# Contractions over 448 rows in chunks of 128, 128, 128 and 64 instead of four of 112, in a fused attention and spatial-gating block

## The chip, the cores and the metric

The kernel runs on one core of a Trainium2 chip. The metric is the device time of one execution in microseconds (us). A run also reports the mean clock that TensorE was granted, as a share of full speed, and a state: slow when it lies over 1.5% above the fastest run of the same kernel, else fast. Comparisons use fast runs; a quoted median is of all runs, and where slow ones are among them the text says so. Where a ratio is quoted, it is the mean time of one kernel's fast runs over that of the other's fast runs of the same rounds, so it isn't quite the ratio of the medians quoted beside it. Engines are called as in the profile: PE (TensorE matmuls), PEld (its weight loads), DVE (VectorE), ACT (ScalarE), POOL (GpSimd), SP (SyncE, which issues all transfers but that of the vector `c`).

## The reference, cut to what matters

```python
# x: 1 x 2048 x 448;  D = 448, 16 heads of 28, a causal window of 256
mod = (silu(c) @ w_mod).reshape(1, 6, 1, 448)        # sa, ca, ga, sb, cb, gb
h = layernorm(x) * (1 + ca) + sa
x = x + ga * A(h)       # qkv = h @ wqkv; masked softmax(q k^T / sqrt(28)) v; @ wo
h = layernorm(x) * (1 + cb) + sb
x = x + gb * B(h)       # z = gelu(h @ w_in); g = w_sp @ layernorm(z2) + b_sp; (z1 * g) @ w_out
```

Every product with `w_mod`, `wqkv` and `wo` contracts over D = 448 rows. Each is done as four matmuls that accumulate into one result. How 448 is split over the four is what the change alters. In the second half (`B`) the split over 448 was 128, 128, 128, 64 already, and there the left-over 64-row matmuls are few.

## The kernel before

A planner lays out all operations per engine from a list of priorities, and emits each engine's program with semaphores. The parts that matter, with cuts marked:

```python
KP = 112; KC = 4                              # 448 = 4 x 112
WARM = (15, 5)                                # warm-up matmuls: at the start, behind the modulation
# ...
def wload(name, prio, dst, w, a, b, o=None, ks=(0, KC), eng="sp"):
    src = w[ks[0] * KP:ks[1] * KP, a:b].rearrange("(c p) n -> p c n", p=KP)
    return load(name, prio, lambda e: e.dma_start(dst[0:KP, ks[0]:ks[1], o:o + b - a], src), ...)
# ...  modulation columns: 448 x 1 results, in groups of four one-column matmuls
for kc in range(KC):
    last = mm(e, ps[0:w, b, 4 * i + mc:4 * i + mc + 1],
              wmod_sb[0:KP, kc, v * D + mc * KP:v * D + mc * KP + w],
              sc_sb[0:KP, kc:kc + 1], kc == 0, kc == KC - 1)
# ...  queries and keys: 48 groups of four
return mm(e, ps[:, ten.slot, 0:n], WQK[0:KP, kc, 4 * g:4 * g + 4, :].rearrange("p a b -> p (a b)"),
          hT[0:KP, kc, t0 * 128:t1 * 128], kc == 0, kc == KC - 1)
# ...  values: 16 groups
return mm(e, ps[:, ten.slot, 0:D], hT[0:KP, kc, t * 128:(t + 1) * 128], wv_sb[0:KP, kc, :], kc == 0, kc == KC - 1)
# ...  attention output: 16 groups
return mm(e, ps[:, wt.slot, 0:D], oT[0:KP, oTt.slot, kc, :], wo_sb[0:KP, kc, :], kc == 0, kc == KC - 1)
```

The softmax here doesn't subtract the row's maximum and nothing guards it: scores larger than these inputs give would overflow.

## Time and profile before

| | before |
|---|---|
| time, median (range), in the runs of the comparison | 283.23 us (282.51 to 283.36) |
| span of the profiled run, granted clock | 280.8 us, 0.999 |
| PE busy | 268.1 us |
| first / last exponential starts | 16.02 / 112.84 us |
| changes of TensorE's tile shape, in program order | 123 |

How to read it: three stretches follow each other. Up to 16 us the inputs land, the modulation is computed and the first queries and keys are projected. From there to the last exponential (90 of them on ACT) is the attention. The rest is the second half, almost pure TensorE. The profile's lines stand in the prediction. The row that is last counts how often the next matmul uses a tile of another shape than the one before (128, 64 or 32 rows; in 3 of the 123 cases only the columns differ). The text calls this a mode change; by the records of this run, one between row counts adds 91 to 96 ns (medians) to the spacing of two starts. Scores run on 32 rows (the heads are padded to 32), nearly everything else on 112 or 128, which count as one shape: a matmul of 128 rows starts as soon behind one of 112 as behind another of 128 (at 448 columns 189 ns in both cases).

### The profile page before, as it was taken

The numbers are of one execution on the slowest core, as the hardware profiler recorded it, in microseconds if no ns is written. First come the engines' busy times: TensorE is split into PE (matmuls) and PEld (weight loads), VectorE is DVE, ScalarE is ACT, GpSimd is POOL, SyncE is SP. The second block draws the span as 40 slices with busy tenths as digits, with TensorE's granted clock in tenths as the row PEclk, the third lists the DMA queues.
The fourth block names the chain that finished last, engine by engine and source line by source line (L and its number), as shares of the span: only waits on it lengthen the run. The fifth ranks groups of instructions, "written<-read, shape, count | busy, mean of one in ns | idle before, by whom it ended". The sixth has DMA issues, their size and how long they took to land.

```text
span 280.8 us, 6444 instructions
## 1 busy us (share of the span) xinstructions
PE 268.1 (95%) x2669; PEld 136.8 (49%) x2684; DVE 173.1 (62%) x439; ACT 128.1 (46%) x171; POOL 64.7 (23%) x110
## 2 busy tenths in 40 slices
PE   7879998999999989999989999999999999999995
PEld 2656755645555745534334344444444444454452
DVE  4599869768787898999888712232314044425335
ACT  4388899999999998936654500002000000000000
POOL 5041425454544748113131300000000000000000
PEclk9999999999999999999999999999999999999999
DMA  6994272963484466668999994000000000011113
GB/s 168 270 267 80 57 134 40 161 69 23 86 144 98 105 92 124 96 136 134 183 204 183 187 194 75 2 0 0 2 0 0 0 2 0 0 33 52 34 33 114
DMA packets 66300, 25.15 MB, mean 90 GB/s; under 512 B 57504, under 2 KB 65632, under 8 KB 66272
## 3 DMA queue, kind: packets, MB, share of 16 engines
q1 hardware_dynamic: 66144, 24.75, 46.3%
q8 instruction: 21, 0.34, 0.6%
q14 instruction: 7, 0.06, 0.1%
q10 hardware_dynamic: 128, 0.00, 0.0%
HBM read 9.01 MB, written 1.84 MB: 39 GB/s over the span
## 4 chain that ended last, share of the span: by engine, by line
PE 80%; ACT 7%; DMA 6%; DVE 3%; issue 2%; SPq 0%; DVEq 0%
PE ps L1940 80%; ACT PT L2172 6%; DMA oT<-o_sb 3%; DMA wqk_raw<-in_A_wqkv_dram 3%; DVE hT L2076 1%; ACT QKT L2110 1%; DVE Vaug L2133 1%; DVE o_sb L2205 0%; ACT hT L2060 0%; SPq L1878 0%; DVE WQK L2086 0%; DVE QKT L2113 0%; DVE fin L2405 0%; DVE hT L2064 0%; DVE rec_all L2202 0%
## 5 line engine op out<-in xcount | busy, mean ns | idle before, releaser
L2172 ACT ACTIVATE PT<-ps 128x1024 bf16<-128x1024 f32 x90 | 84.8, 1046 | 5.3 <-PE ps L1940 4.9
L1940 PE MATMUL ps<-w_spA,z 128*128 128x512 bf16 x329 | 76.4, 379 | 0.4
L2383 DVE TENSOR_TENSOR tmpg<-ps,bsp_bc 128x512 bf16<-128x512 f32 x28 | 19.3, 691 | 65.9 <-PE ps L1940 65.9
L1940 PEld LDWEIGHTS ps<-w_spA,z 128*128 128x128 bf16 x336 | 32.8, 98 | 39.6 <-PE ps L1940 0.4
L2181 POOL TENSOR_SCALAR_AFFINE_SELECT PT<-PT 128x512 f32<-128x512 f32 x60 | 38.3, 646 | 41.3 <-ACT PT L2172 41.1
L2010 POOL TENSOR_TENSOR rs_all<-ve_all,neghalf 128x1 f32<-128x1 f32 (+2 forms) x39 | 24.3, 631 | 54.3 <-DVE ve_all L2008 52.0
L1940 PE MATMUL ps<-hT,WQK 112*128 112x256 bf16 (+1 forms) x192 | 33.9, 308 | 2.5 <-ACT hT L2060 0.9
L2362 ACT ACTIVATE z1T<-ps 128x512 bf16<-128x512 f32 x28 | 14.4, 611 | 39.5 <-PE ps L1940 39.5
L1940 PE MATMUL ps<-w_spB,z 128*128 128x512 bf16 x109 | 27.8, 379 | 0.1
L1940 PE MATMUL ps<-hT,w_in_sb 128*128 128x512 bf16 (+1 forms) x108 | 23.0, 380 | 1.3 <-PE ps L1940 1.0
L1940 PE MATMUL ps<-w_in_sb,hT 128*128 128x448 bf16 (+1 forms) x128 | 24.2, 353 | 0.0
L1940 PE MATMUL ps<-w_out_sb,z1T 128*128 128x448 bf16 x112 | 22.0, 352 | 0.0
L1940 PEld LDWEIGHTS ps<-hT,WQK 112*128 112x128 bf16 x192 | 16.6, 97 | 11.2 <-PE ps L1940 2.8
L1940 PE MATMUL ps<-Vaug,PT 128*128 128x29 bf16 x720 | 21.8, 175 | 0.1
L1940 PEld LDWEIGHTS ps<-Vaug,PT 128*128 128x128 bf16 x720 | 20.3, 97 | 3.1 <-PE ps L1940 0.4
L2014 DVE BATCH_NORM_STATS2 st_all<-x_sb 128x6 f32<-128x448 bf16 x32 | 19.4, 616 | 2.5 <-DMA x_sb<-in_A_x_dram 2.4
L1940 PE MATMUL ps<-QKT 32*128 32x128 bf16 x720 | 18.2, 216 | 1.9 <-ACT PT L2172 1.2
L2113 DVE CAST QKT<-ps 128x512 bf16<-128x512 f32 (+1 forms) x27 | 15.3, 569 | 6.4 <-PE ps L1940 6.3
L1940 PEld LDWEIGHTS ps<-QKT 32*128 32x128 bf16 x720 | 10.7, 92 | 16.1 <-PE ps L1940 13.6
L1940 PEld LDWEIGHTS ps<-w_spB,z 128*128 128x128 bf16 x112 | 10.9, 98 | 13.2
L1940 PE MATMUL ps<-wo_sb,oT 112*128 112x448 bf16 x64 | 15.7, 352 | 1.3 <-DMA oT<-o_sb 1.0
L1940 PEld LDWEIGHTS ps<-w_in_sb,hT 128*128 128x128 bf16 (+1 forms) x128 | 9.8, 97 | 13.1 <-issue 3.5
(58 smaller groups left out, 240.0 us busy)
## 6 DMA issues: line engine op xcount, KB each, us to landing
w_in_sb<-in_B_w_in_dram SPq DMA_DIRECT2D x8, 224.0 KB, 4.5
out_dram<-fin SPq DMA_DIRECT2D x16, 112.0 KB, 1.7
x_sb<-in_A_x_dram SPq DMA_DIRECT2D x3, 448.0 KB, 10.1
wmod_sb<-in_w_mod_dram SPq DMA_DIRECT2D x6, 196.0 KB, 3.8
wmod_sb<-in_w_mod_dram SPq DMA_DIRECT2D x1, 784.0 KB, 7.0
wqk_raw<-in_A_wqkv_dram SPq DMA_DIRECT2D x2, 392.0 KB, 8.3
w_out_sb<-in_B_w_out_dram SPq DMA_DIRECT2D x3, 224.0 KB, 3.1
bsp_bc<-in_B_b_sp_dram SPq DMA_DIRECT2D x1, 512.0 KB, 5.4
```

Of the source, the lines that this page charges most:

```text
L1940: return e.matmul(out_, lhsT=lhsT, rhs=rhs, start=st, stop=sp, **kw)
L2010: return P.op(name + "rs", prio, [("pool", 515 + 150 * (t1 - t0 - 1), lambda e: e.tensor_tensor(rs_all[:, slot, t0:t1], ve_all[:, slot, t0 ...
L2014: st = [P.op("%sst%d" % (name, i), prio, [("dve", dve_ns(D, base=65), lambda e, i=i, s_=s_: e.bn_stats(st_all[:, slot, t, i, :], s_()))], ...
L2076: return e.tensor_scalar(hT[0:KP, cc, t0 * 128:t1 * 128], hT[0:KP, cc, t0 * 128:t1 * 128], modT[0:KP, 4 + cc:5 + cc], modT[0:KP, cc:cc + 1 ...
L2110: return e.activation(QKT[:, g, t0 * 128:t1 * 128], ps[:, ten.slot, 0:n], ACT.Copy)
L2113: return e.tensor_copy(QKT[:, g, t0 * 128:t1 * 128], ps[:, ten.slot, 0:n])
L2133: return e.tensor_copy(Vaug[:, t, :, 0:DH], ps[:, ten.slot, 0:D].rearrange("p (h d) -> p h d", d=DH))
L2172: return e.activation(PTb[:, pt.slot].rearrange("p g q i -> p (g q) i"), ps[:, ten.slot:ten.slot + 2, :].rearrange("p i n -> p n i"), ACT. ...
L2181: return e.affine_select(out=v, in_=v, pattern=[[0, 4], [s_, 128]], compare_op=ALU.is_ge if diag else ALU.is_gt, fill=0.0, base=0, channel ...
L2362: z1_op[(ft, tb)] = P.op("z1g%d_%d" % (tb, ft), pr, [("act", act_ns(512), lambda e, tb=tb, ft=ft, ten=ten: e.activation(z1T[:, ft, tb * 51 ...
L2383: a = P.op("ga%d_%d" % (tb, ft), pr, [("dve", 610, lambda e, tb=tb, ten=ten, tg=tg: e.tensor_tensor(tmpg[:, tg.slot, :], ps[:, ten.slot, : ...
```

## The change

Its intent: six sevenths of each weight are fetched over all 128 partitions, and no longer all of it over 112, so that weights land earlier; three of four matmuls of a contraction then also run on 128 rows. With it come a new layout of the vector `c`, more warm-up behind the modulation, and a newly tuned plan (priorities and release points, some 1,480 lines of the diff). The core, with cuts marked:

```diff
-    KP = 112
+    rows = lambda k: 128 if k < 3 else 64
-WARM = (15, 5)
+WARM = (14, 4, 4)
@@ loads: 128 partitions x 3 chunks, then 64 partitions
+        return [load(name + "a", prio, lambda e: e.dma_start(dst[:, 0:3, o:o + n], src0), 3 * 128 * n * 2),
+                load(name + "b", prio + 0.001, lambda e: e.dma_start(d3, s3), 64 * n * 2)]
@@ queries and keys (values, output, gates and modulation columns likewise)
-                    return mm(e, ps[:, ten.slot, 0:n], WQK[0:KP, kc, 4 * g:4 * g + 4, :].rearrange("p a b -> p (a b)"),
-                              hT[0:KP, kc, t0 * 128:t1 * 128], kc == 0, kc == KC - 1)
+                    return mm(e, ps[:, ten.slot, 0:n], WQK[0:rows(kc), kc, 4 * g:4 * g + 4, :].rearrange("p a b -> p (a b)"),
+                              hT[0:rows(kc), kc, t0 * 128:t1 * 128], kc == 0, kc == KC - 1)
@@ ... c as one row, turned by four one-column matmuls; two SiLU; evacuations in 128 and 64 rows; PLAN ...
```

## The prediction

Passages that no trace or run of this case shows are cut from the recorded text below, and marked. In point (1), which comes from the trace of the kernel before like the others, "such changes" are changes of the tile's shape from one matmul to the next; point (2) gives mean times of one weight load by its rows. +0.6 in the head, +4.2 from 16 to 40 us, +4.6 from 40 to 109 and +0.6 later are the +10.0, less 2.0 by choice, thus +8.0 us. Within the head's term the rates of the new loads are estimates of mine: 375 GB/s on 128 partitions from the 378 measured with x, and 250 at best on 64 from the 250 measured with weights on 112; the rate of a transfer on 64 partitions was not read from the trace. And how much busy time flatters: from 40 to 109 us the records have PE busy for 65.7 us, of which the starts leave 56.0 for streaming.

> **What bounds the kernel now.** I read the page first, then busy time in stages, then the timeline of single instructions, then the transfers of the first 22 us. The page and its chain of waits name TensorE:
>
> ```profile
> PE 268.1 (95%) x2669; PEld 136.8 (49%) x2684; DVE 173.1 (62%) x439; ACT 128.1 (46%) x171; POOL 64.7 (23%) x110
> ...
> PE 80%; ACT 7%; DMA 6%; DVE 3%; issue 2%; SPq 0%; DVEq 0%
> ```
>
> In the second line 80% of the chain that ended last is matmuls. Busy time flatters a pipelined engine, so I also took the start of each matmul and subtracted the time that its columns stream, which in unbroken sequences is 109 ns for 256 columns, 189 for 448 and 216 for 512. What is left over is stall or reconfiguration. From 162 us to the end this leaves 2.2 us in 119: a solid stretch that the change doesn't touch. The attention stage before it, where the change acts, is narrower than it looks:
>
> ```profile
> 40.00:60.00 20.00, 18.56 (x372) 10.66 (x368) 16.53 (x40) 19.87 (x22) 10.35 (x16) 1.00 0.67 98
> 60.00:80.00 20.00, 19.74 (x373) 10.77 (x372) 15.63 (x34) 19.14 (x22) 10.77 (x17) 1.00 0.36 62
> 80.00:100.00 20.00, 19.34 (x443) 12.04 (x436) 16.79 (x50) 19.56 (x23) 10.70 (x18) 1.00 0.65 112
> ```
>
> The columns are PE, PEld, DVE, ACT and POOL busy, then the clock. The reader is to see two engines near full at once: ACT 19.1 to 19.9 of 20 us, with exponentials, and PE. By matmul starts, PE has from 40 to 109 us 56.0 us of streaming, 6.9 of reconfiguration and only 6.2 of stall. From 11 to 40 us it stalls 2.8 us, and from 0 to 11 us 4.5.
>
> [...] (1) [...] This trace has such changes: score matmuls of 32 rows, and the 64-row remainders of the second half's projections. The weight loads around one such remainder:
>
> ```profile
> 112.39 0.29 PEld L1940 LDWEIGHTS ps<-w_in_sb,hT 128*128 128x128 bf16 x2
> 113.04 0.11 PEld L1940 LDWEIGHTS ps<-w_in_sb,hT 64*128 64x128 bf16 x4 [0.37 <-issue]
> 113.53 0.30 PEld L1940 LDWEIGHTS ps<-w_in_sb,hT 128*128 128x128 bf16 x3 [0.37 <-PE ps L1940]
> ```
>
> The loads stand still 0.37 us on both sides of the four 64-row ones. In the matmuls the last 128-row one starts at 112.76 and the first 64-row one at 113.05 us, 0.285 us later in the records instead of 0.189; the way back is 0.285 as well. Over the trace, the 14 changes from 128 to 64 rows have a median of 96 ns over the streaming time, the way back 92 ns, and those to and from 32 rows 92 to 96 and 91. So one change costs 94 ns[...].
> (2) [...] 97 ns for 112 rows, 98 for 128, 94 for 64. So the shorter last chunk saves nothing, and the four matmuls of a contraction stay four.
> (3) [...] The weights lie on 112 partitions, the input x on 128:
>
> ```profile
> 8.50:9.00 0.50, 0.50 (x27) 0.50 (x23) 0.00 (x0) 0.00 (x0) 0.00 (x0) 1.00 1.09 254
> 9.00:9.50 0.50, 0.42 (x12) 0.38 (x10) 0.00 (x0) 0.00 (x0) 0.00 (x0) 1.00 1.08 251
> ...
> 11.50:12.00 0.50, 0.50 (x7) 0.45 (x6) 0.50 (x3) 0.24 (x1) 0.00 (x0) 1.00 1.09 378
> ```
>
> The last column is GB/s. Packets of weights (112 partitions) move about 250 GB/s, those of x (128) up to 378, with the engines equally full. In the packet records an 896-byte packet takes 41 ns in x and 56 to 67 in weights.
>
> **The change part by part.**
> *Loads.* Up to the query/key weights the queue carries x (0.23 MB) and 1.61 MB of weights. At 240 GB/s, as the weight packets came from 3.2 to 9.9 us, the weights take 6.7 us. Afterwards six sevenths go to 128 partitions, 1.38 MB at about 375 GB/s (3.7 us), and one seventh to 64 partitions, 0.23 MB at 250 GB/s at best (0.9): 4.6 us. So the query/key weights should be in about 2.1 us earlier, and the modulation weights, half of it, about 1.0. The later loads (value weights, now ahead of the second x load, and the gate) come earlier still. Extra transfers cost about 0.5 us of SP each, hidden while the queue is full.
>
> *The vector c* now comes as one row, is turned by four one-column matmuls behind c's 2.3 us landing, and goes through two SiLU. All this fits in front of the modulation weights, which land at 8.3 us now and at about 7.3 afterwards: nothing on the path.
>
> *Warm-up* goes from 20 to 22 matmuls. Clock is already granted in full before 8 us, and they fill the hole behind the modulation: nothing.
>
> *Contractions.* Every group of four now ends in a 64-row matmul. No tile position is written for it. The present kernel's 64-column modulation matmuls, without one either, start 93 ns after the one before instead of 25, so I assume that the small shape picks the 64-row mode by itself. There are 48 query/key groups, 16 value, 16 output, 2 gates and 18 modulation columns. I walked the present order of matmuls, marked the last of each group as 64-row and counted mode changes: 123 become 286. 163 more, at 94 ns, are **15.3 us** of TensorE. By stage: 1.5 us before 11 us (modulation), 1.2 from 11 to 16 (first query/key block), 4.9 from 16 to 40, 7.1 from 40 to 109 and 0.6 later. Changing the row split elsewhere (normalized tiles now contiguous, pads of another shape) keeps instruction counts and widths.
>
> **What lies on the path.** The head today:
>
> ```profile
> 8.31 1.06 PE L1940 MATMUL ps<-sc_sb,wmod_sb 112*128 112x1 bf16 x32 [0.28 <-DMA wmod_sb<-in_w_mod_dram]
> ...
> 9.85 0.70 DVE L2086 COPY WQK<-wqk_raw 112x896 bf16<-112x896 bf16 x2 [2.76 <-DMA wqk_raw<-in_A_wqkv_dram]
> ...
> 11.32 3.67 PE L1940 MATMUL ps<-hT,WQK 112*128 112x256 bf16 x32 [0.63 <-DVE hT L2064]
> ...
> 16.02 1.94 ACT L2172 ACTIVATE PT<-ps 128x1024 bf16<-128x1024 f32 x2 [0.60 <-PE ps L1940]
> ```
>
> The modulation would start 1.0 us earlier but take 1.5 longer. The DVE copies, which hold its evacuation up today, come earlier, so the first query/key matmul moves perhaps 0.5 us forward; its 32 matmuls then need 3.7 + 1.2 us. The first exponential, at 16.0 now, comes at about 16.6: the loads' gain is used up: +0.6. From 16 to 40 us, 4.9 us of changes meet 2.1 us of stalls, of which I let 0.7 absorb changes: +4.2. From 40 to 109 us, 7.1 us meet stalls of 6.2, but ACT also needs 97% of the time from 40 to 100, so stalls are mostly the price of two engines handing work over; I let 2.5 us be absorbed: +4.6. Later +0.6. The sum is +10.0. Earlier x and value loads relieve DVE, which is full from 14 to 21 us (6.96 of 7), and the schedule is newly tuned; for both I take off 2.0 us, a choice and not a measurement: **+8.0 on 283.2, thus 291.2 us**.
>
> **Rivals.**
> A: *The loads win.* The head shrinks by up to 2 us, mode changes vanish in PE's stalls, or the new order puts 64-row matmuls side by side. For it: the stalls between 0 and 109 us add up to 13.4 us. Against it: 163 changes need 15.3, and ACT is full as well. It would give 279 to 283.
> B: *No mode change happens,* as the small chunk runs in the full mode. For it: no tile position is given. Against it: the 93 ns above. Then only the head counts: 281 to 283.
> C: *Nothing is absorbed.* All 15.3 us arrive, less about 1.5 of loads: 297. For it: TensorE is the bound almost everywhere. Against it: the stalls above are real and some are waits for ACT, which has time to catch up when PE is slower.
> D: *More waits from reordering.* If the tuned schedule is made without the price of these changes, its order on ACT and DVE is off in time, and buffers come free late: 293 to 296.
>
> **Range and chances.** A and B give the low end, C and D the high one. I predict 291.2 us, 8 in 10 between 285.0 and 296.0. Over 2% slower is above 288.9, over 2% faster below 277.6. Faster 0.03; within 2% 0.22 (A, B, or more absorption than I think); slower 0.75.
>
> **What would show it.** Right: query/key, value and output matmuls in two forms, 128 and 64 rows; weight loads idle around the 64-row ones as above; some 280 mode changes; query/key weights landing near 9.4 us and the first exponential not before 16; attention ending some 8 us later; from 162 us of today on, the same 119 us. Wrong: 64-row matmuls starting 189 ns behind their neighbours (B), or 64-row matmuls lying next to each other (A), or a first exponential under 14.5 us. If attention stretches by more than the changes on PE explain, D.

## The result, and the profile after

| | before | after |
|---|---|---|
| time, median (range) | 283.23 us (282.51 to 283.36) | 294.04 us (292.95 to 294.29) |
| span, granted clock of the profiled run | 280.8 us, 0.999 | 292.1 us, 0.987 |
| changes of tile shape | 123 | 291 |
| modulation columns start / last | 8.31 us / 1.06 us | 6.99 us / 2.23 us |
| first query/key matmul; the 32 of the first block take | 11.32 us; 3.67 us | 11.41 us; 5.29 us |
| first / last exponential | 16.02 / 112.84 us | 18.15 / 122.18 us |

Four fast runs on each side; the ratio is 1.038, 95% interval 1.035 to 1.041. The changed kernel is slower, by 10.8 us between the medians.

The page of the changed kernel, the lines of PE's busy time, of the clock in 40 slices of the span, and of the chain that ended last:

```profile
PE 282.3 (97%) x2663; PEld 136.3 (47%) x2690; DVE 174.0 (60%) x441; ACT 131.1 (45%) x171; POOL 64.1 (22%) x111
...
PEclk9999999999999999599999999999999999999999
...
PE 89%; DVE 4%; DMA 2%; ACT 2%; issue 1%; SPq 1%
```

PE's busy time rose by 14.2 us for the same mathematics, and its share of the chain from 80 to 89%: nothing else became the bound, PE itself needs longer. The 5 in the clock's row was not there before: around 120 us TensorE had half its clock.

How the time gets into PE shows at a value group in the timeline of weight loads. Columns are start, busy time, engine, source line, operands, tile rows*columns, shape, count; in brackets the idle time before.

```profile
16.64 0.30 PEld L1962 LDWEIGHTS ps<-wqkv_raw,hT 128*128 128x128 bf16 x3
17.31 0.09 PEld L1962 LDWEIGHTS ps<-wqkv_raw,hT 64*128 64x128 bf16 x1 [0.37 <-issue]
17.60 0.23 PEld L1962 LDWEIGHTS ps<-QKT 32*128 32x128 bf16 x16 [0.20 <-PE ps L1962]
```

The load for the 64-row chunk waits 0.37 us with nothing named as its releaser but its own issue. Measured on the matmuls that follow, a change from 128 to 64 rows adds 96 ns to the spacing of two starts, the way back 102 to 104 ns, and in the one-column matmuls of the modulation 71 and 82 ns.

The head of the changed kernel, the same four stations as in the prediction:

```profile
6.99 2.23 PE L1962 MATMUL ps<-sc_sb,wmod_sb 128*128 128x1 bf16 x32
...
9.18 1.29 DVE L2111 COPY WQK<-wqkv_raw 128x896 bf16<-128x896 bf16 x4 [2.05 <-DMA wqkv_raw<-in_A_wqkv_dram]
...
11.41 5.29 PE L1962 MATMUL ps<-hT,WQK 128*128 128x256 bf16 x32 [0.37 <-ACT hT L2085]
...
18.15 1.93 ACT L2197 ACTIVATE PT<-ps 128x1024 bf16<-128x1024 f32 x2
```

The modulation weights land 1.8 us earlier (6.5 against 8.3 us by the transfers in the trace), their matmuls start 1.3 us earlier, and the copies of the query/key weights start 0.7 us earlier. Both gains are gone at the first query/key matmul (11.41 against 11.32 us), and 32 of these take 1.6 us longer.

The attention in stretches of 20 us (PE, PEld, DVE, ACT, POOL busy, clock, transfers), to be held against the three lines in the prediction:

```profile
40.00:60.00 20.00, 19.68 (x355) 11.04 (x354) 13.05 (x28) 18.01 (x21) 8.62 (x13) 1.00 0.46 92
60.00:80.00 20.00, 19.40 (x319) 9.23 (x320) 12.72 (x26) 17.88 (x19) 7.60 (x12) 1.00 0.90 146
80.00:100.00 20.00, 18.80 (x395) 10.57 (x393) 18.35 (x50) 18.91 (x21) 12.51 (x21) 1.00 0.56 91
```

ACT falls from 58.6 to 54.8 of these 60 us: it waits for PE now. The two engines are no longer level; PE, busy for 57.9 us of them, alone sets the pace.

And the half clock, in the same columns (the last but two is the clock):

```profile
112.00:116.00 4.00, 4.00 (x61) 2.29 (x49) 3.75 (x11) 3.67 (x5) 1.78 (x3) 1.00 0.62 152
116.00:118.00 2.00, 2.00 (x35) 1.56 (x35) 0.85 (x7) 0.45 (x2) 0.21 (x1) 0.77 0.32 63
118.00:120.00 2.00, 2.00 (x33) 0.91 (x32) 1.69 (x5) 0.99 (x1) 1.43 (x3) 0.50 0.36 87
120.00:122.00 2.00, 1.52 (x42) 1.18 (x40) 1.30 (x4) 1.77 (x2) 0.86 (x2) 0.50 1.03 221
122.00:124.00 2.00, 2.00 (x7) 0.77 (x6) 1.89 (x8) 1.98 (x3) 1.65 (x3) 0.52 0.52 89
124.00:126.00 2.00, 2.00 (x13) 0.78 (x11) 2.00 (x7) 0.70 (x2) 0.14 (x1) 1.00 0.32 62
```

PE is busy in all of these but for 0.48 us after 120 us, yet from 117.09 to 123.92 us it had half its clock. From 114.36 to 117.17 us, directly ahead and without a pause, lie the 40 one-column matmuls of the second modulation, with one other matmul among them. The stretches of one clock in this trace and in that of the kernel before, but for the last of each, which the end of the record cuts off, are whole multiples of 3.413 us, which the text calls a window: the stretch at half clock lasts 6.827 us, two of them, and starts 112.64 us, 33 of them, after the first grant of the full clock; the full clock behind it lasts 167.25 us, 49, and in the kernel before 273.07 us, 80. The trace doesn't show an idle PE ahead of the stretch: what runs there is busy by the records, but streams one column at a time.

### The profile page after: what moved, and what is told of

Its sections match the earlier page's. It is cut to its first block, busy times and chain, and to the rows that moved or that the text cites. A ratio compares the mean times of both kernels' runs of the same rounds, so it can differ in the third digit from the quotient of the medians.

```text
span 292.1 us, 6449 instructions
## 1 busy us (share of the span) xinstructions
PE 282.3 (97%) x2663; PEld 136.3 (47%) x2690; DVE 174.0 (60%) x441; ACT 131.1 (45%) x171; POOL 64.1 (22%) x111
## 4 chain that ended last, share of the span: by engine, by line
PE 89%; DVE 4%; DMA 2%; ACT 2%; issue 1%; SPq 1%
PE ps L1962 89%; DMA wqkv_raw<-in_A_wqkv_dram 2%; ACT PT L2197 2%; DVE st_all L2039 1%; DVE hT L2101 1%; ACT hT L2085 1%; DVE WQK L2111 0%; DVE o_sb L2230 0%; DVE x_sb L2246 0%; DVE rec_all L2227 0%; DVE fin L2430 0%; ACT QKT L2135 0%; SPq L1885 0%; DVE QKT L2138 0%; SPq L1892 0%
## 5 line engine op out<-in xcount | busy, mean ns | idle before, releaser
L2197 ACT ACTIVATE PT<-ps 128x1024 bf16<-128x1024 f32 x90 | 86.6, 1026 | 8.4 <-PE ps L1962 7.3
L1962 PE MATMUL ps<-hT,WQK 128*128 128x256 bf16 (+3 forms) x181 | 38.5, 307 | 2.3 <-PE ps L1962 1.0
L2035 POOL TENSOR_TENSOR rs_all<-ve_all,neghalf 128x1 f32<-128x1 f32 (+2 forms) x39 | 23.6, 616 | 57.4 <-DVE ve_all L2033 52.5
L1962 PEld LDWEIGHTS ps<-hT,WQK 128*128 128x128 bf16 (+1 forms) x192 | 15.0, 96 | 21.7 <-issue 12.5
L1962 PE MATMUL ps<-hT,w_in_sb 128*128 128x512 bf16 (+1 forms) x107 | 24.0, 385 | 0.7 <-DVE st_all L2039 0.5
L2138 DVE CAST QKT<-ps 128x256 bf16<-128x256 f32 (+1 forms) x29 | 15.9, 551 | 9.1 <-PE ps L1962 8.7
L1962 PE MATMUL ps<-wo_sb,oT 128*128 128x448 bf16 x64 | 17.5, 366 | 0.3 <-DVE o_sb L2230 0.3
L1962 PE MATMUL ps<-wqkv_raw,hT 128*128 128x448 bf16 (+1 forms) x64 | 17.2, 356 | 0.0
```

Of the source, the lines that this page charges most:

```text
L1962: return e.matmul(out_, lhsT=lhsT, rhs=rhs, start=st, stop=sp, **kw)
L2035: return P.op(name + "rs", prio, [("pool", 515 + 150 * (t1 - t0 - 1), lambda e: e.tensor_tensor(rs_all[:, slot, t0:t1], ve_all[:, slot, t0 ...
L2138: return e.tensor_copy(QKT[:, g, t0 * 128:t1 * 128], ps[:, ten.slot, 0:n])
L2197: return e.activation(PTb[:, pt.slot].rearrange("p g q i -> p (g q) i"), ps[:, ten.slot:ten.slot + 2, :].rearrange("p i n -> p n i"), ACT. ...
```

## The experiments

Twelve runs, in four sittings; each sitting had its own chip and its own runs of the kernel before. The theory: the added mode changes cost the time, at a price below the 94 ns of each, as some of them fall into waits. Rivals: the new loads and the new plan hold it up (a head that is late by order, not by mode changes), the half clock does it, or the 64-row chunk costs by its shape.

### Only the cut, in the kernel before

The chunk of 112 rows of the fourth matmul is cut to 64, in the kernel before; loads, plan and order stay. It drops rows from the sums (the arithmetic is not the reference's).

```diff
+    kcut = lambda k: KP if k < 3 else 64
-  ... WQK[0:KP, kc, ...], hT[0:KP, kc, ...]
+  ... WQK[0:kcut(kc), kc, ...], hT[0:kcut(kc), kc, ...]     # values, output, gates, modulation likewise
```

> The kernel before, with its loads, schedule and order of instructions as they are; only the last of the four chunks of every contraction over D is cut from 112 to 64 rows in the matmul (the result is wrong on purpose). Mode changes of TensorE go from 123 to 286. Theory (each change of the row mode costs about 94 ns on a TensorE that has little slack): 292 to 296 us. Rival 1 (the new loads and the newly tuned schedule cost the time, mode changes hide in stalls): 283 to 285 us. Rival 2 (the drop of the clock to one half near 117 us of the changed kernel is the larger part): below 287 us, or it shows the same drop.

Measured: 299.08 us median of four (295.1 to 300.82, two of them slow) against 282.56; the two fast runs are 295.1 and 298.24 us, ratio 1.049 (1.040 to 1.058). The second lies above the 292 to 296 that I expected; its mean clock of 0.971 is five windows at half clock, where the first (0.987) has two. The kernel before, with nothing changed but the rows that its fourth chunks read, is as slow as the changed one and slower. Its mode changes are 286. So neither the loads nor the plan is needed to explain a loss. Its profile has half clock for 6.8 us as well, directly behind the same one-column matmuls (102.5 to 104.4 us, half clock from 104.56).

### The 64-row chunk run on 128 rows, in three portions

The changed kernel keeps loads, plan and order, but the matmuls read all 128 rows of the fourth chunk, with zeros in rows 64 to 127, which a few memsets lay down at the start. The work streamed is the same; only the mode changes go. First in queries, keys, values and output, then everywhere, then in the modulation and the gates alone.

```diff
+        e.memset(WQK[:].bitcast(F32)[64:128, 3, :, 0:DH // 2], 0.0)     # hT, wqkv_raw, wo_sb, wmod_sb likewise
-  ... WQK[0:rows(kc), kc, ...], hT[0:rows(kc), kc, ...]
+  ... WQK[:, kc, ...], hT[:, kc, ...]
```

> The changed kernel with the last chunk of the query/key, value and output contractions run over 128 rows, of which 64 hold zeros in both operands (four small memsets on VectorE in an idle hole at the start). Loads, schedule and order stay. Mode changes fall from 291 to 161. Theory: 130 changes of 94 ns are 12.2 us of TensorE, of which 8 to 11 us return: 283 to 286 us. Rival 1 (loads and schedule): 292 to 294 us.

> As the run before, with the last chunk of the modulation columns and of the gates padded to 128 rows too: 128 mode changes against 123 of the kernel before. Theory: what is left is the loads and the new schedule alone; the head is 1 to 2 us shorter than in the kernel before, so 280 to 283 us, and the clock does not drop in the middle. Rival 1: 292 to 294 us. Rival 2 (the drop of the clock comes from the schedule, not from the mode changes): the drop near 117 us stays and costs 2 to 3 us, so 283 to 286 us.

> The changed kernel with only the modulation columns and the gates padded to 128 rows; query/key, value and output keep their 64-row chunk. 258 mode changes against 291. Theory: 33 changes at 70 to 96 ns are 2.3 to 3.2 us of TensorE, of which about 2 return: 291 to 292.5 us. If the mode changes among the one-column matmuls of the second modulation are what makes the clock drop to one half near 117 us, the drop goes and a further 2 to 3 us return: 288.5 to 290 us. If the drop stays: 291 us or more.

| version | mode changes | time, median (range) | ratio to before (95%) | clock in its runs |
|---|---|---|---|---|
| padded everywhere | 128 | 281.45 us (281.1 to 282.73) | 0.996 (0.992 to 1.000) | 1.0 in all four |
| padded in queries to output | 161 | 284.79 us (282.75 to 284.86) | 1.005 (0.999 to 1.010) | 0.986 to 1.0 |
| padded in modulation and gates | 258 | 290.3 us (289.93 to 290.85) | 1.027 (1.023 to 1.031) | 1.0 in all four |

The padded version is back at the time of the kernel before, with every other part of the change in it. The total is as expected, but my reason for it, a head shorter by 1 to 2 us, is not: its first exponential starts at 16.89 us against 16.02 before, and the gain is there only by the sixteenth (38.05 against 40.19 us). By the starts of its matmuls PE streams 244.7 us in it, as in the changed kernel: these 64-row chunks, run alone, save nothing against 128 rows (where two of them meet in the changed kernel, at 13.95 and 30.08 us, they start 119 and 120 ns apart at 256 columns, full ones 109). From 128 to 258 changes, both at full clock, the time grows by 290.3 - 281.45 = 8.85 us: 68 ns realised for each of the 130 changes, about 70% of what each costs on PE. What is left from 290.3 to the changed kernel's 294.04 is 3.7 us for 33 changes, most of them among one-column matmuls, and the half clock.

The page of the padded version, profiled again in the next sitting, with the lines of PE and of the clock:

```profile
PE 267.4 (96%) x2663; PEld 137.2 (49%) x2690; DVE 174.6 (62%) x447; ACT 128.7 (46%) x171; POOL 64.4 (23%) x111
...
PEclk9999999999999999999999999999999999999999
```

And its weight loads for the first query/key and value matmuls:

```profile
12.39 2.84 PEld L1973 LDWEIGHTS ps<-hT,WQK 128*128 128x128 bf16 x27 [0.39 <-ACT hT L2096]
15.25 0.58 PEld L1973 LDWEIGHTS ps<-wqkv_raw,hT 128*128 128x128 bf16 x4
```

27 and 4 loads follow without a pause where the changed kernel stopped 0.37 us for one, and PE's busy time is that of the kernel before again.

### Loads and order, on top of the padded version

Three kernels on one chip, five rounds: the padded version once more, the same with two things moved in the plan, and the same with later weights. The moves put the evacuation of the modulation columns ahead of the four copies of the query/key weights on DVE, and the first tile's value matmuls behind the first scores. The late loads come from a useless transfer of 0.57 MB placed between the first tiles of x and the modulation weights.

```diff
+    # after planning: 'modAe*' before the first 'wqkc*'; 'v0_*' behind 'S0_0'
```

```diff
+            if a == 0:
+                e.dma_start(w_out_sb[:, 0:5, :], B_w_out...[:, 0:5, :])    # 0.57 MB, loaded again later
```

> The padded version once more, as the reference of the next two on the same chip. Both theories: 281.5 us again (281.0 to 282.0), ratio to the kernel before 0.992 to 1.0, no half-clock stretch, 128 mode changes.

> The padded version, with the evacuation of the modulation columns moved ahead of the four copies of the query/key weights on VectorE, and the value matmuls of the first tile moved behind the first score matmuls. Theory that the new order holds the head up: the first query/key matmul and the first exponential come 1.0 to 1.5 us earlier than in the padded version (16.9 there), and the whole takes 280.0 to 281.0 us. Rival, that the stretch up to the fifteenth exponential is set by VectorE or TensorE work whatever the order: first exponential earlier, the fifteenth (38.05 us) and the total within 0.3 us of the padded version.

> The padded version with 0.57 MB of a later weight loaded once more between the first x tiles and the modulation weights, so that the modulation and query/key weights land about 1.5 us later, about when the kernel before has them. Engine orders unchanged. Theory that early landing is worth little because the head is then set by VectorE and TensorE: total at most 0.5 us above the padded version. Rival, that the loads' gain is what the padded version lives on: first exponential and total 1.2 to 1.8 us later, thus about 283 us.

| version | first exponential | time, median (range) | ratio to before (95%) |
|---|---|---|---|
| padded | 16.75 us | 281.45 us (280.91 to 282.06) | 0.993 (0.990 to 0.996) |
| padded, reordered | 18.09 us | 281.58 us (281.03 to 283.21) | 0.994 (0.991 to 0.998) |
| padded, later loads | 18.75 us | 282.66 us (281.9 to 283.13) | 0.997 (0.993 to 1.001) |

The reordering is a miss: its first exponential came later, not earlier, and the time stayed. Two lines of its timeline, a copy on DVE and the first scores on PE:

```profile
10.22 1.29 DVE L2122 COPY WQK<-wqkv_raw 128x896 bf16<-128x896 bf16 x4 [0.70 <-DMA wqkv_raw<-in_A_wqkv_dram]
...
16.34 0.40 PE L1973 MATMUL ps<-QKT 32*128 32x128 bf16 x16 [0.57 <-DVE ve_all L2044]
```

The evacuation did move up, but in that run the copies then waited for the query/key weights themselves, and the scores, without the value matmuls in front, stand 0.57 us. (The releaser named, `ve_all`, is not an input of theirs; the last evacuation of queries and keys that they read ends on ACT at 16.20 us.) The planned order had filled that wait. The later first exponential is in part chance: by the same transfers the weights landed 0.9 us later in this profile than in that of the padded version (10.2 against 9.3 us). So the totals judge the order, and they are equal; my theory that it holds the head up finds no support. (The 38.05 us of the expectation is the start of the sixteenth exponential, not the fifteenth.)

The later loads missed my expectation too, in the other direction:

```profile
9.25 1.05 PE L1981 MATMUL ps<-sc_sb,wmod_sb 128*128 128x1 bf16 x32 [1.91 <-DMA wmod_sb<-in_w_mod_dram]
```

The modulation began 1.4 us later (9.25 against 7.88 us), the first exponential 2.0 us, and the whole took 1.2 us more, where I had allowed 0.5. So later loads do delay the head and the whole. But the transfer delayed them by more than the change had won: the kernel before starts its modulation at 8.31 us and its copies of the query/key weights at 9.85, this version at 9.25 and 11.22. Of the padded version's 2.0 us gain over the kernel before in this sitting, the earlier landing is therefore at most about 1.2 us; how much less isn't shown.

### The warm-up, and the reordering in the changed kernel itself

The changed kernel with two warm-up matmuls behind the modulation instead of eight; and, with its 64-row matmuls in place, with the same two moves as above.

```diff
-            for _ in range(n):
+            for _ in range(n if first else 1):      # warm1, warm2: one matmul each
```

> The changed kernel with two warm-up matmuls behind the modulation instead of eight; the planned order is kept. My theory of the prediction, that these only fill a hole: 293.5 to 294.5 us, clock in the head unchanged. Rival, that they guard the clock after the one-column matmuls: a half-clock stretch of 3.4 or 6.8 us between 9 and 18 us and a total 1.5 to 3 us longer.

> The changed kernel with all its 64-row matmuls, but the evacuation of the modulation columns ahead of the copies of the query/key weights on VectorE, and the first tile's value matmuls behind the first score matmuls. Theory, that about 1.5 us of the first exponential's delay (18.15 us against 16.0 before) come from this order: first exponential at 16.2 to 17.2 us, total 292.5 to 293.5. Rival, that the head is late because of mode changes alone: first exponential not before 17.6 and the total within 0.3 us of 294.0. If the total stays while the first exponential moves, the stretch after it is set by other work.

Fewer warm-ups: 297.85 us median (294.76 to 300.34, the highest of them slow and the profiled one), ratio of the fast runs 1.049 (1.044 to 1.054). My reading of the prediction, that the warm-up only fills a hole, is wrong. In the profile of its slow run:

```profile
10.00:12.00 2.00, 1.63 (x11) 0.84 (x11) 2.00 (x9) 1.22 (x3) 0.00 (x0) 0.67 1.11 322
12.00:16.00 4.00, 4.00 (x18) 1.55 (x17) 2.12 (x6) 1.14 (x4) 0.70 (x1) 0.50 1.13 317
...
28.00:30.00 2.00, 2.00 (x40) 1.21 (x39) 1.09 (x4) 1.57 (x3) 0.00 (x0) 1.00 0.01 4
```

Half clock from 10.67 to 27.74 us, five windows, and the 32 query/key matmuls take 8.46 us instead of 5.29. So the eight warm-ups help to keep the clock up behind the modulation, which with its mode changes lasts 2.2 us instead of 1.1. They don't always: of the six profiles that have both these mode changes and all eight warm-ups, three (padded in queries to output, the reordered changed kernel and the one with full matmuls below) show one window of half clock there, from 10.93, 10.62 and 10.23 us. Of its five fast runs four have a mean clock of 0.971, five windows, and take 297.26 to 298.39 us; the fifth has 0.983, three windows, and takes 294.76.

The reordered changed kernel took 295.0 us (292.73 to 296.03), ratio 1.040 (1.035 to 1.044): no gain, and a first exponential at 21.18 us in a profile that had one window of half clock in the head. The changed kernel itself was not run in this sitting; its ratios of 1.038 and 1.035 come from others. Again there is no sign that the order is the cause.

### The clock and the count, separately

Three more on one chip, five rounds: the changed kernel again; the changed kernel with 64-row matmuls brought side by side; and the changed kernel with useless full-width matmuls among the one-column ones of the second modulation. In the second, where a group of four follows another on PE, it begins with its 64-row chunk, so that one pair of changes goes; the order of the groups on every engine is the same, and the count falls from 291 to 243.

```diff
+    # after planning: if the matmul before on PE is a 64-row one, run this group as 3, 0, 1, 2
+                    m[i].fn = lambda e, f=fns[kc], kc=kc, i=i: f(e, kc, i)
```

```diff
+                    for _ in range(2):          # behind each of the ten column groups of the second modulation
+                        last = mm(e, ps[:, ten.slot, 16:16 + D], wmod_sb[:, 0, v * D:v * D + 128], wmod_sb[:, 0, v * D:(v + 1) * D], True, True)
```

> The changed kernel once more, as the reference of the next two on the same chip, and for more runs with their granted clock: 292.5 to 295 us, mean clock 0.985 to 0.995, and the longer times with the lower clock (in the earlier versions 1.4 to 1.7 us for each 3.4 us at half clock).

> The changed kernel with the same order of groups on every engine, but wherever two groups of four follow each other on TensorE, the second begins with its 64-row chunk, so that two 64-row matmuls lie side by side; the modulation columns take turns in the same way. 243 mode changes instead of 291, everything else as in the changed kernel. Theory that the count of changes sets the time (68 ns realised for each): 48 x 68 ns = 3.3 us less, and the one-column bursts become shorter, so that the half-clock stretch behind them may go too: 288 to 291 us. Rival, that 64-row chunks cost by themselves (loads, evacuation shapes): within 1 us of the changed kernel.

> The changed kernel with two useless matmuls of 448 columns after each of the ten column groups of the second modulation: 20 x 187 ns = 3.7 us of added TensorE work, three more mode changes, every other engine as before. Theory that the half-clock stretch comes from TensorE streaming too little during these columns, and costs 2 to 3 us: no half-clock stretch there and a total only 0.5 to 1.8 us above the changed kernel. Rival, that the stretch has another cause or costs nothing: it stays, or goes without a gain, and the total is 3 to 4 us longer.

| version | mode changes | time, median (range) | ratio to before (95%) | clock in its runs |
|---|---|---|---|---|
| changed | 291 | 292.6 us (292.31 to 293.95) | 1.035 (1.032 to 1.038) | 0.987 once, else 0.994 |
| paired | 243 | 289.7 us (289.37 to 291.68) | 1.025 (1.022 to 1.028) | 0.988 to 1.0 |
| full matmuls in the modulation | 294 | 295.83 us (295.58 to 297.69) | 1.046 (1.043 to 1.050) | 1.0 in four of six, else 0.994 |

Pairing is worth 2.9 us for 48 changes, 60 ns for each, with every 64-row matmul still there. So what costs is not the chunk but the changes to its neighbours. In its weight loads a query/key and a value group meet:

```profile
63.90 0.09 PEld L1962 LDWEIGHTS ps<-hT,WQK 64*128 64x128 bf16 x1 [0.42 <-issue]
63.91 0.10 PEld L1962 LDWEIGHTS ps<-wqkv_raw,hT 64*128 64x128 bf16 x1
64.41 0.30 PEld L1962 LDWEIGHTS ps<-wqkv_raw,hT 128*128 128x128 bf16 x3 [0.40 <-issue]
```

One idle stretch ahead of the two 64-row loads and one behind, where two such chunks apart have two each. The second half of both kernels goes further: it puts its 64-row remainders in turn on rows 0 to 63 and 64 to 127 of the array (`tile_position=(p0, 0)` in the code), and pairs of them start 4 ns apart in the trace, at 125.589 and 125.593 us in the changed kernel, so that two such matmuls take the time of one (the next pair starts 196 ns later). The chunks of the change all lie on rows 0 to 63; this was not tried for them.

With full matmuls in the modulation the half clock behind it is gone, over the very stretch where the changed kernel had it:

```profile
116.00:118.00 2.00, 2.00 (x28) 1.34 (x21) 1.92 (x8) 1.87 (x2) 1.10 (x2) 1.00 0.77 203
118.00:120.00 2.00, 2.00 (x19) 1.20 (x18) 0.00 (x0) 0.07 (x1) 0.00 (x0) 1.00 0.56 100
120.00:122.00 2.00, 2.00 (x21) 1.28 (x18) 0.00 (x0) 0.00 (x0) 0.00 (x0) 1.00 0.24 58
```

So the half clock there comes from what PE runs in that burst, one column at a time, and not from anything else at that point of the program; why such a burst is followed by half clock, no run shows. The version padded in modulation and gates, with 33 mode changes fewer, most of them in its one-column bursts, kept the full clock in all four runs. It does not pay: I added 3.7 us of matmuls and the total rose by 3.2, more than the 0.5 to 1.8 I had expected and within what the rival expected. On this chip the changed kernel mostly lost one window and not two, so that 3.7 less about 1.5, thus 2.2 us, was to be had; the remaining 1.0 us is not explained.

What a window costs can be read from runs of one kernel that differ in their clock; one window at half clock in 292 us lowers the mean by 0.5 x 3.413 / 292 = 0.006. The changed kernel's nine runs in two sittings fall in two groups: five at 0.994, mean 292.63 us, and four at 0.987 or 0.988, mean 294.08. The difference is **1.45 us for one window**. In the version with full matmuls it is 1.8 us (295.7 at 1.0, 297.5 at 0.994). Not one of the nine runs kept the full clock; of the 40 runs of the kernel before in the four sittings, 11 lost one window or two.

## Why the prediction was right

The predicted 291.2 us is 2.8 us under the measured 294.04, inside the range, on the side given 0.75. The mechanism was the one named: the small shape runs on a 64-row tile without being told to (64*128 in the records), which makes two mode changes per group (291 in all, at 96 to 104 ns each among the large matmuls). Put together from the medians above (283.23 before, 281.45 padded, 290.3 padded in the modulation alone, 294.04 after; other chips, so good to about a microsecond: the medians of the kernel before alone range from 282.56 to 283.41):

| term | predicted | measured | from |
|---|---|---|---|
| mode changes added, on PE | 163 x 94 ns = 15.3 us | 15.9 us | the changed trace against the one before |
| of these absorbed by waits | -3.2 us (0.7 and 2.5) | about -6.3 us (-5.4 within one pair of traces) | 15.9 less the two parts that arrive: 8.85 (130 changes) and 0.8 (33) |
| loads, head and plan together | -4.1 us (2.1 in the head, 2.0 as a choice) | -1.8 us | 283.23 to 281.45 |
| half clock | 0 | 2 x 1.45 = 2.9 us | the two groups of runs |
| sum | +8.0 us | +10.7 us | measured +10.8 us |

The 0.8 us is 290.3 to 294.04 less the 2.9 us of clock, an estimate that rests on the price of a window. The measured column adds up by construction, as its parts are differences of the same medians, so its sum is no check; the -5.4 from one pair of traces is one, for the absorption.

**The count and the price.** 286 changes predicted, 291 there; 94 ns predicted, 96 to 104 measured in the large matmuls. Rival B (no mode change happens) is refuted by the weight loads and by the padded version. Rival C (nothing is absorbed, 297 us) fits neither 60 nor 68 ns realised of about 97. Rival A (the loads win, 279 to 283 us) needed the changes to vanish in stalls or by the order; 291 are there and the time rose.

**The absorption** was mis-sized, in one stretch of two. I let 0.7 of 4.9 us be absorbed from 16 to 40 us and 2.5 of 7.1 from 40 to 109. The changed kernel against the padded one, which has the same order, gives for the profiled runs of the second and the fourth sitting: up to the first exponential 29 more changes (2.5 us of PE) and 2.0 us of time; from there to the sixteenth 35 changes (3.4 us) and 1.5 us; from the sixteenth to the last 97 changes (9.3 us) and 8.0 us, or 6.5 without the window of half clock that lies in it. So from the sixteenth on 70% arrive, near the 65% that I had reckoned with, though the new plan has put more changes there. Between the first and the sixteenth only 44% arrive and not 86%: later loads cost there too (1.5 us of the late-load run's 2.0 are left at the sixteenth), so PE is not alone in setting that pace, which would make a slower PE cost less; this reason is argued, not tested. Within this pair 5.4 us are absorbed for the 3.2 predicted, and this stretch is 1.2 of the 2.2 us between them.

**The head** failed more. Landing was about right: the modulation weights were predicted at 7.3 and landed at 6.5 us; the query/key weights at 9.4, and their two parts landed at 9.15 and 9.7 (the last part before: 11.5), though the queue moved 230 to 401 GB/s from 2 to 9 us and not a steady 375. "The first query/key matmul moves perhaps 0.5 us forward" was not: it starts at 11.41 against 11.32 us, as DVE now runs all four copies of the query/key weights (1.29 us from 9.18) ahead of the modulation's evacuation, where the kernel before ran two. That the modulation's 32 columns last twice as long doesn't decide it: with them back at 1.05 us, in the padded version, the matmul starts at 11.58 us. The first exponential, predicted at 16.6, came at 18.15 us: the 32 matmuls take 1.6 us longer for the 1.2 I had reckoned, and four value matmuls stand in front of the first scores. That this order was a mistake of the plan finds no support in the totals of two runs; it fills a wait.

**The 2.0 us taken off by choice** for loads and plan: with the head's 2.1 us it came to 4.1, and the padded version shows 1.1 us in one sitting and 2.0 in another, of which the late-load run leaves at most about 1.2 to the loads. 2 to 3 us of the 4.1 were counted in vain.

**The warm-up**: "they fill the hole behind the modulation: nothing" was wrong, as taking six of them away costs 3 to 4 us by the ratios (1.049 against 1.035 to 1.038). I had seen the clock granted in full before 8 us and concluded that it stays so. **The half clock** in the middle is the same oversight: I priced the modulation's changes as PE time and did not ask what a longer burst of one-column matmuls does to the clock. Without it, 294.04 would be 291.1 us, so that the predicted number owes its closeness to luck: two errors of size, 3.1 us in the absorption and 2.3 us in the loads, nearly cancel.

**Rival D** (waits from reordering) is not supported: the whole new plan is in the padded version, which is no slower than the kernel before, and two pieces of order moved back by hand changed nothing, there or in the changed kernel. The rest of the order was not tested together with the mode changes. What stays open is how much of the gain over the kernel before, 1.1 or 2.0 us by sitting, is the plan rather than the loads.

The version that beats both kernels is the padded one: 281.45 us, ratio to the kernel before 0.993 (0.990 to 0.996) in the second sitting, though with 0.996 (0.992 to 1.000) in the first.

## What to carry to other kernels

Before splitting a contraction unevenly, count how often the row count changes from one matmul to the next on TensorE, in program order, and price each change at about 97 ns, of which some 60 to 70 ns arrived here, where TensorE was the bound most of the time. If uneven loads are wanted, keep the loads and pad the short chunk with zeros, since a matmul on 64 rows, run alone, took no less time here than one on 128 (119 and 120 ns against 109 at 256 columns); or, where padding is not possible, let neighbouring groups meet at their short chunks. Long bursts of one-column matmuls are not only slow: here 40 of them in 2.8 us, with mode changes among them, cost the clock of the stretch behind them (half of it for 6.8 us), so look at the granted clock by slices and not only at the busy time.
